# The norm's vector folded into the gate and value weights, and the factors of the tokens applied on ScalarE

## The chip, the core and the metric

The kernel runs on one core of one Trainium2 chip. The core has five engines with a queue of instructions each: TensorE (PE, matrix products, with its weight loads as PEld), VectorE (DVE), ScalarE (ACT), GpSimd (POOL), and SyncE (SP), which here only issues DMAs. An engine runs its queue in order and waits on semaphores for the others. The metric is the device time of one execution in microseconds (us). Before the change it is 991.82 us, the median of 3 runs (989.93 to 992.64).

## The reference

Three layers run one after the other over 2,304 tokens of width 512 (18 tiles of 128 tokens).

```python
x = attention(q, k, v)            # window of 128, 8 heads, a bias that falls with distance
# a layer of 8 experts, each token goes to its two best, with weights top2_w
for e in range(E):
    for k in range(2):
        h = np.maximum(x[mask] @ w1[e], 0.0)
        out[mask] += top2_w[mask, k, None] * (h @ w2[e])
# gated layer
rms = np.sqrt(np.mean(x * x, axis=-1, keepdims=True) + 1e-06)
xn = x / rms * rms_g
g = xn @ w_gate
silu = g * (1.0 / (1.0 + np.exp(-g)))
val = xn @ w_val
return (silu * val @ w_out).astype(np.float32)
```

The change concerns the step between the experts and the gated layer (the weighted sum of a token's two expert outputs, and the norm), and the preparation of `w_gate` and `w_val`.

## The kernel before

Products are made from two fp16 parts of each operand: a high part `hi` (ScalarE, a copy with a scale) and a rest `lo` (VectorE or GpSimd, a subtraction), three products of parts for one product.

**Stages.** Attention runs first, then the experts 0 to 7, with the experts' and the gated layer's weights split into parts beside the products. `m2_part` (L638 to L646) lists the 36 pieces of the gated layer's weights, `m2_steps` (L648) decodes and splits them: ScalarE writes `hi` at L658 with the scale `sc`, VectorE writes `lo` at L661. The gated layer then works on a first block of 2 token tiles (`FIRST`) and four blocks of 4 tiles (`QT`). The first block goes through `gated` (L853): 12 chunks f0 to f11 of 128 columns of the hidden width. The four later blocks go through `quads` (L965 to L1043), which needs fewer products but needs sums of weight blocks (`weight_sums`, L922: VectorE adds at L933, ScalarE copies at L936, GpSimd subtractions at L939). Most of these sums are made while the first block and the start of block 1 run.

**One chunk of `gated`.** TensorE makes the gate product and the value product (L875) into two PSUM rings, `mm0` with 3 buffers and `mm1` with 2. ScalarE writes silu of the gate product into a tile `gt` (even chunks) or `vt` (odd chunks), at L880. VectorE multiplies by the value product (L887), ScalarE copies that to `pgh` (L889), VectorE subtracts to `pgl` (L891). Each of `gt` and `vt` has one buffer, so silu of chunk f+2 waits for L891 of chunk f, and TensorE's value product of chunk f+2 waits for L887 of chunk f.

**Tokens for the next block.** `combine` (L792) runs for a block while the block before it is computed. In steps it gathers the two expert outputs of a token tile with two indirect DMAs of GpSimd (`ya`, `yb`, L758), then makes `ya*cw0` (L764) and `yb*cw1 + ya` (L765) on VectorE (`mixed`), the sum of squares on ScalarE (L719), the inverse root (L723 to L738), and for two pairs of tiles the norm (L741, VectorE: `ya*r*gb`, with `gb` the vector `rms_g` on all partitions, times 4), four additions (L818 to L821), fp16 parts (ScalarE L832, GpSimd L833) and transposing DMAs (L838). `combine_first` (L768) does this for the first block, one tile at a time, during the last expert, with a simpler end: norm, copy to fp16 (L746), a subtraction (L747), a transposing DMA (L748).

**What sets the order.** Everything is issued in the order in which the Python program writes it (`manual_schedule`). `drive` (L146) lets a main generator yield, and each yield tells how many columns TensorE was given. A side generator starts at a column count and then takes one step for each so many columns. `combine` of the first call starts `AHEAD[0]*PACE[0]` = 13*4,000 columns before the end of `gated`, later calls `AHEAD[1]*PACE[1]` = 9*8,000 columns before the end of a block's quads. `combine_first` has a pace of 3,100 columns, `weight_sums` one of 3,200.

Of the kernel before, what the change touches and what calls it, by code (L numbers as in the profile page):

```python
# [13 lines left out]
F32 = mybir.dt.float32  # L14
# [7 lines left out]
P = 128  # L22
# [5 lines left out]
MM = (3, 2)  # L28
VN = 96

AHEAD, PACE = (13, 9), (4000, 8000)

SOON, SUM0, SUMS = 3, 6000, 3200

# [7 lines left out]
def attention_moe_swiglu(  # L42
# [49 lines left out]
    over = consts.tile([P, 1], I32, name="over")  # L92
    tops = consts.tile([P, NT, 2], F32, name="tops")

    gb = consts.tile([P, DM], F32, name="gb")
    wts = {}

    def weight_steps(epools, stage, w1, w2, ws):
# [140 lines left out]
    with ExitStack() as actx:  # L239
# [169 lines left out]
        def constants():  # L409
            nc.vector.tensor_scalar(wgh, wg, SG, None, op0=OP.mult)  # L410
            nc.vector.scalar_tensor_tensor(wgl, wg, SG, wgh, op0=OP.mult, op1=OP.subtract)
            yield
            nc.vector.tensor_copy(bias[1], bias[0])
            nc.gpsimd.memset(bias[1][P // 2:, :, :P + P // 2], NEG * KS)
            yield
            nc.vector.tensor_copy(bias[2], bias[0])
            nc.gpsimd.memset(bias[2][:, :, :P // 2], NEG * KS)
            yield
            nc.gpsimd.memset(ones, 1.0)
            nc.gpsimd.memset(tri, 1.0)  # L420
            nc.gpsimd.affine_select(out=tri, in_=tri, compare_op=OP.is_gt, fill=0.0, base=0,
                                    pattern=[[1, P]], channel_multiplier=-1)
            nc.gpsimd.iota(iota8, pattern=[[1, E]], base=0, channel_multiplier=0,
                           allow_small_or_imprecise_dtypes=True)
            nc.vector.tensor_scalar(gb, gb, SN, None, op0=OP.mult)

            for e in range(E):
                yield
                nc.sync.dma_start(xrows[e * N + CAP - P:e * N + CAP, :], x16s[0].rearrange("p a d -> p (a d)"))
# [31 lines left out]
        def route(t0, nb):  # L461
# [49 lines left out]
            if t0 < 10:  # L511
# [6 lines left out]
            nc.vector.tensor_scalar(rank, rank, float(CAP - 1), None, op0=OP.min)  # L518
            nc.vector.scalar_tensor_tensor(ysl[:, ts, :], ixf, float(CAP), rank, op0=OP.mult, op1=OP.add)

        nc.sync.dma_start(gb, bass.AP(tensor=moe2_rms_g.tensor, offset=moe2_rms_g.offset,
                                      ap=[[0, P], [1, DM]]))
        few = work.tile([P, len(EARLY)], F32, name="few", bufs=1)

        def take(i, tiles, cs):
# [112 lines left out]
    def m2_part(i):  # L638

        if i < 6 * KC:  # L640
            m, j = divmod(i, 3 * KC)
            c, n0 = j // 3, j % 3 * DM
            src, sc = ((moe2_w_gate, SWG), (moe2_w_val, SWV))[m]
            return (src[c * P:(c + 1) * P, n0:n0 + DM], sc, *(x[:, c, n0:n0 + DM] for x in gw[2 * m:2 * m + 2]))
        c = i - 6 * KC
        return moe2_w_out[c * P:(c + 1) * P, :], SWO, ow[0][:, c, :], ow[1][:, c, :]  # L646

# [83 lines left out]
    def inverse(mp, vv, r):  # L731
        nc.vector.reciprocal(r, r)

        u = mp.tile([P, QT], F32, name="u")[:, :r.shape[1]]
        nc.vector.tensor_tensor(out=u, in0=vv, in1=r, op=OP.mult)
        nc.vector.tensor_tensor(out=u, in0=u, in1=r, op=OP.mult)
        nc.vector.tensor_scalar(u, u, -0.5, 1.5, op0=OP.mult, op1=OP.add)
        nc.vector.tensor_tensor(out=r, in0=r, in1=u, op=OP.mult)  # L738

    def normal(x3, r):  # L740
        nc.vector.scalar_tensor_tensor(x3, x3, r, gb, op0=OP.mult, op1=OP.mult)  # L741

    def turned(mp, x3, r, xnT, lo):
        normal(x3, r)
        xn = mp.tile([P, 2 * DM], F16, name="xg", bufs=3)
        nc.vector.tensor_copy(xn[:, :DM], x3)  # L746
        lo.tensor_tensor(out=xn[:, DM:], in0=x3, in1=xn[:, :DM], op=OP.subtract)  # L747
        nc.sync.dma_start_transpose(xnT, xn)  # L748

    def columns(xnT, i):  # L750
# [2 lines left out]
    def gather(mp, t, every=False):  # L753

        rows = yall if every else ybuf[:E * CAP if t >= G else (E - 1) * CAP + GW, :]
        ys = [mp.tile([P, DM], F32, name=name, bufs=bufs) for name, bufs in (("ya", QT), ("yb", 2))]
        for j, y in enumerate(ys):
            nc.gpsimd.indirect_dma_start(  # L758
                out=y, out_offset=None, in_=rows,
                in_offset=bass.IndirectOffsetOnAxis(ap=(slots if every else ysl)[:, t, j:j + 1], axis=0))  # L760
        return ys

    def mixed(t, ya, yb):
        nc.vector.tensor_scalar(ya, ya, cw[:, t, 0:1], None, op0=OP.mult)  # L764
        nc.vector.scalar_tensor_tensor(ya, yb, cw[:, t, 1:2], ya, op0=OP.mult, op1=OP.add)  # L765
        return ya

    def combine_first(mp, xnT):  # L768

        ys = [gather(mp, i) for i in range(FIRST)]  # L770
        for _ in range(WAIT):
            yield

        sqs = [mp.tile([P, 1], F32, name=f"sq{i}", bufs=1) for i in range(FIRST)]
        x3s, rs = {}, {}
        for n in range(2 * FIRST + 3):
            for i in range(FIRST):
                j = n - 2 * i
                if j == 0:
                    x3s[i] = mixed(i, *ys[i])  # L780
                elif j == 1:
                    square(mp, x3s[i], sqs[i])
                elif j == 2:
                    rs[i] = variance(mp, sqs[i])
                elif j == 3:
                    nc.scalar.activation(rs[i][1], rs[i][0], AF.Sqrt)
                elif j == 4:
                    inverse(mp, *rs[i])
                    turned(mp, x3s[i], rs[i][1], columns(xnT, i), nc.vector if i == FIRST - 1 else nc.gpsimd)
            yield  # L790

    def combine(mp, t0, xq):  # L792

        ys, x3s = {}, {}
        pairs = [(j, j + HQ) for j in range(HQ)]
        turn = list(itertools.chain(*pairs))
        sq = mp.tile([P, QT], F32, name="sq")
        for n in range(QT + 3):
            if n < QT:
                ys[n] = gather(mp, t0 + turn[n])  # L800
            if 0 <= n - 2 < QT:
                x3s[turn[n - 2]] = mixed(t0 + turn[n - 2], *ys[n - 2])
            if 0 <= n - 3:
                i = turn[n - 3]
                square(mp, x3s[i], sq[:, i:i + 1])
            yield
        vv, r = root(mp, sq)
        yield
        inverse(mp, vv, r)
        yield  # L810
        K2 = DM // 2
        for j, (a, b) in enumerate(pairs):
            xa, xb = x3s[a], x3s[b]
            tt = mp.tile([P, 3, K2], F32, name="tt", bufs=1)
            normal(xa, r[:, a:a + 1])
            normal(xb, r[:, b:b + 1])
            yield
            nc.vector.tensor_tensor(out=tt[:, 0], in0=xb[:, :K2], in1=xa[:, :K2], op=OP.subtract)  # L818
            nc.vector.tensor_tensor(out=xb[:, :K2], in0=xb[:, K2:], in1=xb[:, :K2], op=OP.subtract)
            nc.vector.tensor_tensor(out=tt[:, 1], in0=xb[:, K2:], in1=tt[:, 0], op=OP.subtract)  # L820
            nc.vector.tensor_tensor(out=tt[:, 2], in0=xa[:, K2:], in1=tt[:, 1], op=OP.subtract)  # L821
            yield
            parts = []
            for x in (xa, xb, tt[:, :2].rearrange("p k d -> p (k d)"), tt[:, 2]):
                n = x.shape[1] // K2
                if n == 2:
                    xn = mp.tile([P, 2 * DM], F16, name="xg", bufs=3)
                else:
                    xn = mp.tile([P, DM], F16, name="xh", bufs=1)
                y = xn.rearrange("p (k h d) -> p k h d", k=n, h=2)  # L830
                x = x.rearrange("p (k d) -> p k d", k=n)
                nc.scalar.activation(y[:, :, 0], x, AF.Copy)  # L832
                nc.gpsimd.tensor_tensor(out=y[:, :, 1], in0=x, in1=y[:, :, 0], op=OP.subtract)  # L833
                parts.append(xn)
            yield
            for k, xn in enumerate(parts):
                nb = xn.shape[1] // P
                nc.sync.dma_start_transpose(xq[:, 8 * k:8 * k + nb, j * P:(j + 1) * P], xn)  # L838
            yield

    def normalize(mp, x3s, xnT):
        sq = mp.tile([P, QT], F32, name="sq")[:, :G]
        for i, x3 in enumerate(x3s):
            square(mp, x3, sq[:, i:i + 1])
        vv, r = root(mp, sq)
        inverse(mp, vv, r)
        for i, x3 in enumerate(x3s):
            turned(mp, x3, r[:, i:i + 1], columns(xnT, i), nc.gpsimd)

    def products(ppool):  # L850
        return [ppool.tile([P, GC, QT * P], F16, name=name) for name in ("pgh", "pgl")]
# [243 lines left out]
    with tc.If(flag):  # L1095
        with ExitStack() as c:
# [18 lines left out]
            ph, pl = products(ppool)  # L1115
            for t in range(0, NT, G):
                xnT = xpool.tile([P, 2 * KC, GW], F16, name="xnT")
                normalize(mp, [mixed(t + i, *gather(mp, t + i, True)) for i in range(G)], xnT)
                for _ in itertools.chain(gated(mp, ph, pl, t, G, xnT), projected(ph, pl, t, G, range(GC))):
                    pass  # L1120

# [40 lines left out]
```

## Time and profile before

| | |
|---|---|
| median of 3 runs | 991.82 us |
| profiled execution, its own time | 997.68 us |
| its span, first to last instruction | 996.0 us |
| granted TensorE clock, mean | 0.986 |
| PE busy | 955.9 us (96%) |
| DVE busy | 656.4 us (66%) |
| ACT busy | 450.9 us (45%) |
| POOL busy | 212.0 us (21%) |

All rows come from one profiled execution; their times count from its first instruction. L and a number is a line of the kernel before. In a timeline or an issue order, `out<-in` names tiles. "Idle before, releaser" is the time in which an engine had nothing to run, and what ended it. The granted clock is a share of full speed: 1.00 is 2.4 GHz and 0.50 is 1.2 GHz. Attention takes about the first 165 us, the experts run up to 577.5 us, the first block of the gated layer runs to 634.6 us, and the four later blocks to the end.

### The profile page before, as it was taken

The numbers are of one execution on the slowest core, as the hardware profiler recorded it, in microseconds if no ns is written. First come the engines' busy times: TensorE is split into PE (matmuls) and PEld (weight loads), VectorE is DVE, ScalarE is ACT, GpSimd is POOL, SyncE is SP. The second block draws the span as 40 slices with busy tenths as digits, with TensorE's granted clock in tenths as the row PEclk, the third lists the DMA queues.
The fourth block names the chain that finished last, engine by engine and source line by source line (L and its number), as shares of the span: only waits on it lengthen the run. The fifth ranks groups of instructions, "written<-read, shape, count | busy, mean of one in ns | idle before, by whom it ended". The sixth has DMA issues, their size and how long they took to land.

```text
span 996.0 us, 18517 instructions
## 1 busy us (share of the span) xinstructions
PE 955.9 (96%) x7220; PEld 667.4 (67%) x7220; DVE 656.4 (66%) x1503; ACT 450.9 (45%) x920; POOL 212.0 (21%) x255
## 2 busy tenths in 40 slices
PE   7999987999999999999999998889999999999997
PEld 5998885655656565656565685578478658847864
DVE  6688864537666666667675479989548917954850
ACT  8999852434454545454543335335323413432320
POOL 5467643000000000000001355541401140130000
PEclk9999988999999999999999998999999999999999
DMA  7999664748484757575750232311341070122000
GB/s 217 307 239 287 145 186 138 198 131 229 153 227 164 217 170 215 160 206 167 218 149 22 75 105 51 69 53 33 73 98 33 9 161 1 33 60 59 1 13 34
DMA packets 145279, 127.12 MB, mean 128 GB/s; under 512 B 97696, under 2 KB 114848, under 8 KB 145184
## 3 DMA queue, kind: packets, MB, share of 16 engines
q1 hardware_dynamic: 139424, 106.99, 40.1%
q0 software_dynamic: 5760, 18.88, 5.8%
q8 instruction: 58, 0.95, 0.4%
q14 instruction: 37, 0.30, 0.1%
HBM read 76.81 MB, written 26.74 MB: 104 GB/s over the span
## 4 chain that ended last, share of the span: by engine, by line
PE 86%; DVE 7%; ACT 2%; DMA 2%; issue 1%; SPq 1%; another core or an unknown queue 0%; DVEq 0%; ACTq 0%
PE acc L210 21%; PE mm L189 21%; PE mm L982 21%; PE acc L909 11%; PE acc L361 6%; PE mm L347 3%; DVE sums L933 3%; PE mm L319 2%; DMA xq<-xg 1%; SPq L838 1%; PE mm L875 1%; DVE pgl L891 1%; DMA raw<-in_qkv 1%; PE rt L458 1%
## 5 line engine op out<-in xcount | busy, mean ns | idle before, releaser
L189 PE MATMUL mm<-xT,w1h 128*128 128x256 f16 (+2 forms) x1088 | 167.1, 294 | 1.1 <-issue 0.8
L195 DVE SCALAR_TENSOR_TENSOR hl<-mm,hh 128x256 f16<-128x256 f32 (+2 forms) x136 | 63.5, 469 | 118.8 <-ACT hh L194 117.6
L189 PEld LDWEIGHTS <-w1h 128*128 128x128 f16 x1088 | 104.8, 99 | 41.2 <-issue 2.6
L210 PE MATMUL acc<-w2h,hh 128*128 128x512 f16 x320 | 121.3, 379 | 0.0
L210 PE MATMUL acc<-w2l,hh 128*128 128x512 f16 x320 | 121.3, 379 | 0.0
L210 PE MATMUL acc<-w2h,hl 128*128 128x512 f16 x320 | 121.3, 379 | 0.0
L939 POOL TENSOR_TENSOR sw<-sums,sw 128x256 f16<-128x256 f32 x36 | 28.4, 809 | 391.8 <-ACT sw L936 391.8
L210 PEld LDWEIGHTS <-hh 128*128 128x128 f16 x640 | 62.6, 98 | 72.8
L982 PE MATMUL mm<-xq,sw 128*128 128x256 f16 x864 | 100.4, 273 | 2.4 <-DMA xq<-xg 2.3
L194 ACT ACTIVATE hh<-mm 128x256 f16<-128x256 f32 (+2 forms) x136 | 56.6, 419 | 92.2 <-PE mm L189 86.2
L982 PEld LDWEIGHTS <-sw 128*128 128x128 f16 x864 | 84.3, 98 | 13.0 <-issue 2.7
L189 PE MATMUL mm<-xT,w1l 128*128 128x256 f16 (+2 forms) x544 | 93.1, 293 | 0.0
L909 PE MATMUL acc<-oh__3183,pgl 128*128 128x512 f16 (+2 forms) x228 | 83.3, 368 | 1.6 <-DVE pgl L891 1.6
L909 PE MATMUL acc<-oh__3183,pgh 128*128 128x512 f16 (+2 forms) x228 | 83.3, 368 | 0.4 <-ACT pgh L889 0.4
L909 PE MATMUL acc<-ol__3184,pgh 128*128 128x512 f16 (+2 forms) x228 | 83.3, 368 | 0.0
L909 PEld LDWEIGHTS <-pgh 128*128 128x128 f16 x456 | 44.0, 98 | 49.1 <-ACT pgh L889 0.7
L361 PE MATMUL acc<-v,pf 128*128 128x96 f32 x544 | 73.8, 277 | 2.6 <-issue 2.4
L361 PEld LDWEIGHTS acc<-v,pf 128*128 128x128 f32 x544 | 69.3, 197 | 2.4 <-issue 2.4
L189 PEld LDWEIGHTS <-w1l 128*128 128x128 f16 x544 | 52.5, 99 | 18.1
L339 ACT ACTIVATE pr<-ss,nm 128x256 f32<-128x256 f32 (+1 forms) x144 | 63.1, 488 | 3.2 <-DVE nm L330 2.1
L330 DVE CUSTOM_DVE_ANT_0 ss<-mm,bias 128x256 f32<-128x256 f32 (+1 forms) x144 | 54.2, 397 | 15.2 <-PE mm L319 6.7
L232 ACT ACTIVATE ys<-acc 128x512 f32<-128x512 f32 x40 | 23.8, 594 | 82.7 <-PE acc L210 74.2
(190 smaller groups left out, 1729.0 us busy)
## 6 DMA issues: line engine op xcount, KB each, us to landing
st<-in_moe_w SPq DMA_DIRECT2D x64, 512.0 KB, 4.9
ybuf<-ys SPq DMA_DIRECT2D x40, 256.0 KB, 3.0
raw<-in_qkv SPq DMA_DIRECT2D x17, 512.0 KB, 5.5
st<-in_moe_w_gate SPq DMA_DIRECT2D x12, 512.0 KB, 4.7
st<-in_moe_w_val SPq DMA_DIRECT2D x12, 512.0 KB, 4.3
st<-in_moe_w_out SPq DMA_DIRECT2D x12, 512.0 KB, 4.4
v<-in_qkv SPq DMA_DIRECT2D x18, 279.0 KB, 5.6
out<-ys SPq DMA_DIRECT2D x17, 256.0 KB, 2.1
```

Source lines behind the costliest of these rows:

```text
L189: nc.tensor.matmul(hp[:, :w], w1[:, c, f * P:(f + 1) * P], xT[:, xo + c, cs], start=(n == 0), stop=(n == 3 * KC - 1))
L194: nc.scalar.activation(hh[:, f, hs], hp[:, :w], AF.Relu)
L195: nc.vector.scalar_tensor_tensor(hl[:, f, hs], hp[:, :w], 0.0, hh[:, f, hs], op0=OP.max, op1=OP.subtract)
L210: nc.tensor.matmul(yp, hx[:, f, i * P:(i + 1) * P], w2[:, f, :], start=(n == 0), stop=(n == 3 * FC - 1))
L330: nc.vector.tensor_tensor_reduce(out=d["ss"][:, j, c0:], in0=d["sp"][:, j, c0:], in1=bias[kind][:, heads(d["hp"])[j], c0:], scale=-1.0 / K ...
L339: nc.scalar.activation(d["pr"][:, j, c0:], d["ss"][:, j, c0:], AF.Exp, scale=-1.0, bias=d["nm"][:, j:j + 1])
L347: nc.tensor.transpose(pt[:, j, kk, :], d["pr"][:, j, kk * P:(kk + 1) * P], ident)
L361: nc.tensor.matmul(xps[t, hp // 2][:, h % 4, :VN], ph[:, j, kk, :], v32[t - 1 + kk][:, h * DV:h * DV + VN], start=(kk == k0), stop=(kk == 1))
L909: nc.tensor.matmul(op[:, ds], px[:, f, cs], w[:, f, ds], start=(k == 0), stop=(k == 3 * GC - 1))
L933: nc.vector.tensor_tensor(out=o, in0=x, in1=y, op=op)
L939: nc.gpsimd.tensor_tensor(out=here[k][1], in0=x, in1=here[k][0], op=OP.subtract)
L982: nc.tensor.matmul(pp, w(a, pa, c), xq[:, 4 * b + 2 * pb + c, :], start=(n == 0), stop=(n == 5))
```

## The change

The vector `rms_g` leaves the tokens. It is loaded as 128 x 4 (`gain[:, 0]`, one number for each row of a weight chunk), multiplied by the old constant scales `SWG` and `SWV`, and the 24 pieces of the gate and value weights take it as their scale, one number for each partition. The factor 4 (`SN`) of the tokens goes into the inverse root. The norm of a tile is then a factor for each token alone, and it moves from VectorE to ScalarE, as does the first factor of the weighted sum (`weighted`). In `combine_first` and in the spare path, ScalarE writes `hi` from `x3*r` directly, and VectorE writes `lo` as `x3*r - hi`; the separate norm, the copy and GpSimd's subtraction go. `combine` and `combine_first` have one step more, since `weighted` stands a step ahead of `mixed`; `AHEAD` grows by one each, so that `combine` starts a step earlier. `yb` has 3 buffers for 2.

```diff
-AHEAD, PACE = (13, 9), (4000, 8000)
+AHEAD, PACE = (14, 10), (4000, 8000)
...
-            nc.vector.tensor_scalar(gb, gb, SN, None, op0=OP.mult)
+            nc.vector.tensor_scalar(gain[:, 1], gain[:, 0], SWV, None, op0=OP.mult)
+            nc.vector.tensor_scalar(gain[:, 0], gain[:, 0], SWG, None, op0=OP.mult)
...
-        nc.sync.dma_start(gb, bass.AP(tensor=moe2_rms_g.tensor, offset=moe2_rms_g.offset,
-                                      ap=[[0, P], [1, DM]]))
+        nc.sync.dma_start(gain[:, 0], moe2_rms_g.rearrange("(c p) -> p c", p=P))
...
-            src, sc = ((moe2_w_gate, SWG), (moe2_w_val, SWV))[m]
-            return (src[c * P:(c + 1) * P, n0:n0 + DM], sc, *(x[:, c, n0:n0 + DM] for x in gw[2 * m:2 * m + 2]))
+            src = (moe2_w_gate, moe2_w_val)[m]
+            return (src[c * P:(c + 1) * P, n0:n0 + DM], gain[:, m, c:c + 1], *(x[:, c, n0:n0 + DM] for x in gw[2 * m:2 * m + 2]))
...
-        nc.vector.tensor_tensor(out=r, in0=r, in1=u, op=OP.mult)
-
-    def normal(x3, r):
-        nc.vector.scalar_tensor_tensor(x3, x3, r, gb, op0=OP.mult, op1=OP.mult)
-
-    def turned(mp, x3, r, xnT, lo):
-        normal(x3, r)
+        nc.vector.scalar_tensor_tensor(r, r, SN, u, op0=OP.mult, op1=OP.mult)
+
+    def turned(mp, x3, r, xnT):
         xn = mp.tile([P, 2 * DM], F16, name="xg", bufs=3)
-        nc.vector.tensor_copy(xn[:, :DM], x3)
-        lo.tensor_tensor(out=xn[:, DM:], in0=x3, in1=xn[:, :DM], op=OP.subtract)
+        nc.scalar.activation(xn[:, :DM], x3, AF.Copy, scale=r)
+        nc.vector.scalar_tensor_tensor(xn[:, DM:], x3, r, xn[:, :DM], op0=OP.mult, op1=OP.subtract)
         nc.sync.dma_start_transpose(xnT, xn)
...
-        ys = [mp.tile([P, DM], F32, name=name, bufs=bufs) for name, bufs in (("ya", QT), ("yb", 2))]
+        ys = [mp.tile([P, DM], F32, name=name, bufs=bufs) for name, bufs in (("ya", QT), ("yb", 3))]
...
+    def weighted(t, ya, yb):
+        nc.scalar.activation(ya, ya, AF.Copy, scale=cw[:, t, 0:1])
+
     def mixed(t, ya, yb):
-        nc.vector.tensor_scalar(ya, ya, cw[:, t, 0:1], None, op0=OP.mult)
         nc.vector.scalar_tensor_tensor(ya, yb, cw[:, t, 1:2], ya, op0=OP.mult, op1=OP.add)
         return ya
...
-        for n in range(QT + 3):
+        for n in range(QT + 4):
             if n < QT:
                 ys[n] = gather(mp, t0 + turn[n])
             if 0 <= n - 2 < QT:
-                x3s[turn[n - 2]] = mixed(t0 + turn[n - 2], *ys[n - 2])
-            if 0 <= n - 3:
-                i = turn[n - 3]
+                weighted(t0 + turn[n - 2], *ys[n - 2])
+            if 0 <= n - 3 < QT:
+                x3s[turn[n - 3]] = mixed(t0 + turn[n - 3], *ys[n - 3])
+            if 0 <= n - 4:
+                i = turn[n - 4]
                 square(mp, x3s[i], sq[:, i:i + 1])
...
-            normal(xa, r[:, a:a + 1])
-            normal(xb, r[:, b:b + 1])
+            for i in (a, b):
+                nc.scalar.activation(x3s[i], x3s[i], AF.Copy, scale=r[:, i:i + 1])
```

TensorE's order is the same before and after, and SP's differs in the one load of `rms_g`. Two places of the other engines follow. The first is VectorE's queue during the first block, from L891 of chunk f4 on; `ya` and `yb` are the gathered outputs, `sums` the sums of weight blocks. Before:

```order
L891 TENSOR_TENSOR pgl<-gt,pgh 128x256
L887 TENSOR_TENSOR vt<-vt,mm_7486 128x256
L933 TENSOR_TENSOR sums<-sums 128x256 x2
L764 TENSOR_SCALAR ya<-ya,cw 128x512
L765 SCALAR_TENSOR_TENSOR ya<-yb,cw,ya 128x512
L933 TENSOR_TENSOR sums<-vh__3181,sums 128x256
L933 TENSOR_TENSOR sums<-vl__3182,sums 128x256
L764 TENSOR_SCALAR ya<-ya,cw 128x512
L765 SCALAR_TENSOR_TENSOR ya<-yb,cw,ya 128x512
L891 TENSOR_TENSOR pgl<-vt,pgh 128x256
L887 TENSOR_TENSOR gt<-gt,mm_7532 128x256
```

After, from the pair of additions on:

```order
L936 TENSOR_TENSOR sums<-sums 128x256 x2
L764 SCALAR_TENSOR_TENSOR ya<-yb,cw,ya 128x512
L936 TENSOR_TENSOR sums<-vh__3182,sums 128x256
L936 TENSOR_TENSOR sums<-vl__3183,sums 128x256
L764 SCALAR_TENSOR_TENSOR ya<-yb,cw,ya 128x512
L894 TENSOR_TENSOR pgl<-vt,pgh 128x256
L890 TENSOR_TENSOR gt<-gt,mm_7532 128x256
```

The two products of `ya` with `cw` are gone, and nothing else has moved; the pairs of norms (`ya<-ya,r,gb`) further down are gone from this queue in the same way. The second place is ScalarE's queue a little later, around the table load between the root and the silu of chunk f9. Before:

```order
L728 ACT_TABLE_LOAD
L728 ACTIVATE r<-vv 128x4
L889 ACTIVATE pgh<-vt 128x256
L936 ACTIVATE sw_7249<-sums 128x256
L880 ACT_TABLE_LOAD
L880 ACTIVATE vt<-mm_7664 128x256
L936 ACTIVATE sw_7250<-sums 128x256
L889 ACTIVATE pgh<-gt 128x256
```

After:

```order
L729 ACT_TABLE_LOAD
L729 ACTIVATE r<-vv 128x4
L892 ACTIVATE pgh<-vt 128x256
L939 ACTIVATE sw_7248<-sums 128x256
L883 ACT_TABLE_LOAD
L883 ACTIVATE vt<-mm_7663 128x256
L939 ACTIVATE sw_7249<-sums 128x256
L819 ACTIVATE ya<-ya,r 128x512 x2
L892 ACTIVATE pgh<-gt 128x256
```

The pair of norms now stands on ScalarE between the silu of chunk f9 and the copy `pgh` of chunk f8.

## Rows read from the trace of the kernel before

**Rows 1.** Windows by stage: length, busy by engine, granted clock, DMA share, GB/s.

```profile
300.00:400.00 100.00, 100.00 (x594) 57.91 (x592) 67.17 (x119) 47.72 (x94) 0.00 (x0) 1.00 0.65 189
590.00:604.60 14.60, 10.21 (x93) 8.85 (x92) 13.40 (x24) 5.43 (x18) 10.02 (x11) 0.97 0.42 125
634.60:658.10 23.50, 17.90 (x158) 15.09 (x157) 22.78 (x39) 8.99 (x22) 12.25 (x16) 1.00 0.12 34
658.10:697.90 39.80, 39.80 (x349) 34.98 (x349) 35.39 (x57) 17.69 (x28) 8.56 (x9) 0.96 0.19 54
731.50:785.40 53.90, 53.90 (x493) 48.22 (x493) 44.39 (x69) 20.84 (x33) 2.84 (x3) 1.00 0.07 21
```

**Rows 2.** TensorE's longest waits from 576 to 664: total, times, longest.

```profile
PE mm L982 <- ACT p L1003: 4.1, 2, 2.1
PE mm L875 <- DVE gt L887: 3.1, 1, 3.1
PE acc L909 <- DVE pgl L891: 1.6, 1, 1.6
```

**Rows 3.** Chain that ended last, 590 to 698: start, length, what.

```profile
590.18 0.46 DVE ya L764
...
594.71 0.41 DVE ya L764
...
599.38 1.44 DVE ya L764
...
602.59 0.49 DVE ya L764
...
611.49 1.32 DVE ya L741 x2
...
623.62 1.33 DVE ya L741 x2
...
658.06 39.82 PE mm L982 x348
```

**Rows 4.** POOL's timeline: start, length, operation, idle before.

```profile
599.83 1.51 POOL L939 TENSOR_TENSOR hl<-sums,hl 128x256 f16<-128x256 f32 x2
```

**Rows 5.** VectorE's timeline: the first sum, and the product in a later block.

```profile
591.63 1.26 DVE L765 SCALAR_TENSOR_TENSOR ya<-yb,cw,ya 128x512 f32<-128x512 f32 x1 [0.99 <-DMA yb<-ybuf,ysl]
...
678.13 0.48 DVE L764 TENSOR_SCALAR ya<-ya,cw 128x512 f32<-128x512 f32 x1
```

**Rows 6.** ScalarE's timeline: the second table load, two copies to `pgh`.

```profile
610.44 1.28 ACT L880 ACT_TABLE_LOAD   x1 [1.18 <-DVE pgl L891]
...
612.32 0.41 ACT L889 ACTIVATE pgh<-gt 128x256 f16<-128x256 f32 x1
...
625.65 0.42 ACT L889 ACTIVATE pgh<-vt 128x256 f16<-128x256 f32 x1 [3.53 <-DVE vt L887]
```

**Rows 7.** VectorE's timeline, behind that copy.

```profile
612.76 0.87 DVE L891 TENSOR_TENSOR pgl<-gt,pgh 128x256 f16<-128x256 f32 x1
```

**Rows 8.** ScalarE's groups by shape: count, busy, mean ns, idle before.

```profile
L719 ACT ACTIVATE jk<-ya 128x512 f16<-128x512 f32 x18 | 11.2, 620 | 3.2 <-DVE ya L765 3.0
L339 ACT ACTIVATE pr<-ss,nm 128x256 f32<-128x256 f32 x128 | 57.7, 500 | 3.2 <-DVE nm L330 2.1 <-DVE rs L372 0.8
L1003 ACT ACTIVATE p<-mm 128x256 f32<-128x256 f32 x48 | 18.2, 380 | 81.4 <-PE mm L982 79.8 <-DVE vt L991 1.6
```

**Rows 9.** ScalarE's timeline in block 1: copies behind which the products wait.

```profile
675.64 0.38 ACT L1003 ACTIVATE p<-mm 128x256 f32<-128x256 f32 x1 [2.13 <-PE mm L982]
...
680.23 0.38 ACT L1003 ACTIVATE p<-mm 128x256 f32<-128x256 f32 x1 [0.91 <-PE mm L982]
...
684.81 0.38 ACT L1003 ACTIVATE p<-mm 128x256 f32<-128x256 f32 x1 [0.53 <-PE mm L982]
```

**Rows 10.** SP's timeline at the start: two loads and their issue times.

```profile
4.49 0.94 SPq L399 DMA_DIRECT2D wg<-in_moe_w_gate  x1
...
7.58 3.18 SPq L521 DMA_DIRECT2D gb<-in_moe_rms_g  x1
```

More of the change, by code (lines that the diff above doesn't have):

```diff
@@ L93, in attention_moe_swiglu @@
     tops = consts.tile([P, NT, 2], F32, name="tops")
-    gb = consts.tile([P, DM], F32, name="gb")
+    gain = consts.tile([P, 2, KC], F32, name="gain")
     wts = {}
@@ L775, in combine_first @@
         x3s, rs = {}, {}
-        for n in range(2 * FIRST + 3):
+        for n in range(2 * FIRST + 4):
             for i in range(FIRST):
-                j = n - 2 * i
-                if j == 0:
+                j = n - 2 * i - 1
+                if j == -1:
+                    weighted(i, *ys[i])
+                elif j == 0:
                     x3s[i] = mixed(i, *ys[i])
@@ L788, in combine_first @@
                     inverse(mp, *rs[i])
-                    turned(mp, x3s[i], rs[i][1], columns(xnT, i), nc.vector if i == FIRST - 1 else nc.gpsimd)
+                    turned(mp, x3s[i], rs[i][1], columns(xnT, i))
             yield
@@ L847, in normalize @@
         for i, x3 in enumerate(x3s):
-            turned(mp, x3, r[:, i:i + 1], columns(xnT, i), nc.gpsimd)
+            turned(mp, x3, r[:, i:i + 1], columns(xnT, i))
     def products(ppool):
@@ L1117, in attention_moe_swiglu @@
                 xnT = xpool.tile([P, 2 * KC, GW], F16, name="xnT")
-                normalize(mp, [mixed(t + i, *gather(mp, t + i, True)) for i in range(G)], xnT)
+                ys = [gather(mp, t + i, True) for i in range(G)]
+                for i in range(G):
+                    weighted(t + i, *ys[i])
+                normalize(mp, [mixed(t + i, *ys[i]) for i in range(G)], xnT)
                 for _ in itertools.chain(gated(mp, ph, pl, t, G, xnT), projected(ph, pl, t, G, range(GC))):
```

## The prediction

> **What bounds the kernel now.** I read the windows by stage first. From 300 to 400, with the experts at work, TensorE is busy all 100.00 us, and from 731.5 to 785.4 all 53.90 [rows 1]: there a us saved on VectorE or ScalarE returns nothing. From 634.6 to 658.1 it is otherwise: TensorE works 17.90 of 23.50 us and VectorE 22.78; from 590.0 to 604.6 TensorE has 10.21 of 14.60 and VectorE 13.40 [rows 1]. Next the waits of TensorE in that stretch: the three longest kinds, 4.1, 3.1 and 1.6 us, end with a copy `p` of ScalarE, the product L887 and the subtraction L891 of VectorE [rows 2]. So from about 590 to 658 VectorE's queue sets the pace. Last the chain of waits, which shows which of VectorE's instructions lie on the path: it holds the four products L764 and the four norms L741 of the first block's `combine`, until TensorE starts at 658.06 on 39.82 us of products without a stop [rows 3]. What VectorE loses before 658 moves the end; what it loses later doesn't.
>
> **The change, part by part.**
>
> First factors, 590 to 604. Four L764 leave VectorE: 0.46, 0.41, 1.44 and 0.49 us of the chain [rows 3]. The first returns nothing: the sum behind it then waited 0.99 us for the gather `yb` [rows 5], and that wait only becomes longer. The other three make 0.41 + 1.44 + 0.49 = 2.34. The 1.44 is a stretched one: a later one takes 0.48 [rows 5], and while this one ran GpSimd was at two subtractions, 599.83 to 601.34 [rows 4]. If the stretch of 0.96 passes to the neighbour, 2.34 - 0.96 = 1.38 are left; if the gather comes earlier too, 2.34 + 0.46 = 2.80. I take 2.34, the rows as they stand.
>
> The Trainium skill speaks against that value (GPSIMD Engine Reference, Key points): GpSimd and VectorE share their way into SBUF, and contend where a VectorE instruction has two SBUF inputs or uses two ports. The trace agrees that the product is three times as long beside GpSimd [rows 4, 5]. By that rule the neighbour, a sum with two inputs, inherits the stretch, and the total below would be 1.9 in place of 2.9, so 989.9 us.
>
> On ScalarE each factor now stands in front of a copy `pgh` or a silu, waits there until `ya` has landed, and holds what is queued behind it, for which L891 waits. `ya` is the gather before `yb` and lands earlier; its wait is bounded by none and by the 0.99 seen for `yb` [rows 5]. VectorE has sums of its own to do meanwhile, and I count nothing; without that cover it is up to 0.99.
>
> What such an operation costs on ScalarE isn't shown, since it reads its scale for each partition. A 128x512 one with a constant takes 620 ns; on 128x256, one with a bias for each partition takes 500 and one without 380 [rows 8]. So between 0.62 and 0.62 + 0.12 = 0.74 us; I take 0.74, as the row with a pointer is nearest in kind.
>
> Norms of the first pair of tiles, near 612. 1.32 us leave the chain [rows 3], but this is the place where little comes back. ScalarE loads a table at 610.44, then does a silu and a copy, and `pgh` of chunk f8 runs from 612.32 to 612.73; L891, which needs it, starts at 612.76 [rows 6, 7]. VectorE's two norms fitted under that table load. Without them VectorE arrives 1.32 us earlier and waits. And the two norms on ScalarE are issued between that silu and that `pgh`, which puts `pgh` 2 x 0.74 = 1.48 later. So this pair is worth between -1.48 (all of it a wait) and +1.32 (ScalarE has run ahead far enough). The rows put it near the lower end, because `pgh` and L891 lie 0.03 apart; L891 took a stretched 0.87 there [rows 7] and may run freely when it comes later, so I take -0.8.
>
> Norms of the second pair, near 623.6. 1.33 us leave [rows 3]. ScalarE's two stand before `pgh` of f11, in front of which ScalarE was idle 3.53 us for VectorE [rows 6]; 1.48 fit in. The full 1.33 counts; bounds 0 and 1.33.
>
> Edits at nothing. (a) `combine_first` comes one step of 3,100 columns later. With 348 x 256 columns in 39.82 us [rows 3] that is 1.4 us, and its tail loses a norm and a copy on VectorE. If it comes late, TensorE starts the first block up to 1.4 later, and its waits of 4.1 + 3.1 + 1.6 [rows 2] take that in. (b) The 24 weight pieces with a scale for each partition: 24 x 0.12 = 2.9 us more on ScalarE, in a stage where it is busy 47.72 of 100 and TensorE all 100.00 [rows 1]; uncovered, 2.9. (c) The load of `rms_g` becomes 512 runs of four bytes: its issue lies between 0.94 (the load of `wg`, 512 runs) and the 3.18 of the old one [rows 10]. No step of the chain waits on it; SP reaches the next loads up to 2.2 earlier, which nobody is late for. (d) In the three later runs of `combine`, 4 products at 0.48 and 4 norms of about 0.67 each leave VectorE beside a TensorE without a gap [rows 1, 3, 5]: 3 x 4.6 = 13.8 us less work and no time. (e) Gathers are issued a step earlier and `yb` has a third buffer; GpSimd's queue keeps the same gathers and weight subtractions, two of them in turned order, and loses one subtraction of `combine_first`. SP's queue passes nothing.
>
> The sum: 2.34 - 0.8 + 1.33 = 2.9 us. The profiled execution took 997.68 us for a span of 996.0; it would take 994.8. It lies 5.9 us above the median of the runs, 991.82, from which the same 2.9 leave **988.9 us**.
>
> **The rivals.**
>
> R1, VectorE's saving comes back whole. For it: VectorE is 97% busy from 634.6 to 658.1 (22.78 of 23.50), ScalarE 38% (8.99) [rows 1], so ScalarE may run ahead in the chunks before. Against it: the 0.03 us between `pgh` and L891 [rows 6, 7]. It gives 2.34 + 1.32 + 1.33 = 5.0, so 986.8. If TensorE's clock also stays up behind 658, where 39.8 us were granted 0.96, 39.8 x 0.04 = 1.6 more: 985.2.
>
> R2, ScalarE and GpSimd hand most of it back: the stretch passes on and the first pair is all wait, 1.38 - 1.48 + 1.33 = 1.2, so 990.6; with the waits of the factors for `ya`, nothing. For it: rows 4 and 6. Against it: ScalarE idles long in most chunks (the 3.53 of rows 6).
>
> R3, slower: ScalarE falls behind in the blocks where TensorE has no gap. There two factors come in front of one copy `p`, and one each in front of the next two; the copy waits for TensorE's product with 2.13, 0.91 and 0.53 us of idle time before it [rows 9]. At 0.74 each nearly all fits (1.48, 0.74 and 0.74 against these: 0.21 late). If the moved operations were stretched as L764 was, to 1.44, it would be 0.75 + 0.53 + 0.91 = 2.2 us late a block. Should TensorE feel all of it in three blocks, 6.6 - 2.9 = 3.7 slower: 995.5. It turns slower from about 1.1 us an operation, at which (0.07 + 0.19 + 0.57) x 3 = 2.5 are lost, and all has to reach TensorE. Against it: 18 ScalarE operations of this size take 620 ns in the mean [rows 8], none like 1.44. The Trainium skill has a rule of this kind (ScalarE: Activation LUTs, Rules for kernel authors): multiplications belong on VectorE, not on ScalarE. The trace agrees on the price, 0.48 against 0.62 to 0.74 [rows 5, 8]; by the rule the change loses, by the rows only where ScalarE is the later engine.
>
> **How the numbers follow.** I give the forecast 0.48 (987.4 to 990.4), R1 0.22, R2 0.19 and R3 0.11. What a measurement of this kernel can tell from no change is about 0.3%, here 3.0 us, and the forecast sits on that edge: half of its chance counts as faster. Faster is 0.24 + 0.22 = 0.46, the same 0.24 + 0.19 = 0.43, slower 0.11. The range takes in R1 with the better clock and R2 down to no gain, 985.2 to 991.8, and leaves out R3 and a little at the lower end.
>
> **What would show it.** In the changed kernel's profile, the start on the long run of block 1's products (658.06 before) should lie about 3 us earlier. L891 of chunk f8 should wait 1 to 2.5 us for `pgh` on VectorE, with the two norms just before that `pgh` on ScalarE; without that wait R1 holds. From 590 to 604 TensorE should wait about 2 us less for L887. The last four blocks should keep their lengths (53.9 us of quads each); if one grows by over a us, with TensorE waiting for `p`, R3 holds. A stage before 577 us that changes by over a us would make the whole account wrong, as would a stretch up to 658 that stays as long while VectorE idles less than 3 us more.

## The result, and the profile after

The changed kernel is slower: 1000.22 us, the median of 20 runs (992.78 to 1011.4), against 992.97 us for 20 runs of the kernel before; the ratio is 1.0066, 95% interval 1.0049 to 1.0082. One of the 20, that of 1011.4, was in a slow state of the chip and is left out of the ratio. The forecast was 988.9 us, with a range of 985.2 to 991.8.

The profiled execution took 1003.16 us for a span of 1001.1. To compare it with that of before, the part ahead of the gated layer has to be set aside. First the first gated product of each, before and then after:

```profile
577.54 0.39 PE L875 MATMUL mm<-xq,gh 128*128 128x128 f16 x4
```

```profile
573.51 0.39 PE L878 MATMUL mm<-xq,gh 128*128 128x128 f16 x4
```

The 4.03 us between them arise ahead of the experts' second layers: the first product of an expert's second layer comes at 177.30 and 173.27, and from there to the first gated product both take 400.24. In the other profiled executions below the first gated product lies between 569.73 and 576.11, so this part scatters and is no gain. Everything below is counted from the first gated product: 418.46 us to the end before (996.0 - 577.54), 427.59 after. That is 9.1 us more.

The chain of waits of the changed kernel (start, length, what) shows where they are; `xq` are the transposed tokens of the next block. It answers to [rows 3]:

```profile
588.75 4.42 DMA ya<-ybuf,ysl
...
593.20 0.72 ACT ya L761
...
608.68 1.22 ACT ya L819 x2
609.90 0.32 ACT pgh L892
610.24 0.43 DVE pgl L894
...
653.84 38.15 PE mm L985 x348
691.99 23.32 PE acc L912 x108
...
720.15 9.48 DMA xq<-xg
...
729.68 56.04 PE mm L985 x492
785.72 23.32 PE acc L912 x108
...
814.01 8.38 DMA xq<-xg
...
822.44 55.54 PE mm L985 x492
877.98 31.08 PE acc L912 x144
```

and the same part of the chain before, behind the last of [rows 3]:

```profile
697.87 23.32 PE acc L909 x108
...
726.22 5.22 DMA xq<-xg
...
731.49 53.87 PE mm L982 x492
785.36 23.32 PE acc L909 x108
...
813.62 5.17 DMA xq<-xg
...
818.83 53.87 PE mm L982 x492
```

From the first gated product to the long run of 348 products it took 80.52 us before (658.06 - 577.54) and 80.33 after (653.84 - 573.51): of the 2.9 us forecast, 0.2 came. The 348 products took 38.15 instead of 39.82, 1.7 less, because the clock stayed up (granted 1.00 there, against the 0.96 of [rows 1]). The loss lies behind: from the end of a block's quads to the next block's it took 33.62 us before (731.49 - 697.87) and 37.69 after, then 33.47 and 36.72. That is 4.07 + 3.25 us, and the products behind the two waits took 2.17 and 1.67 longer. The sum is -0.19 - 1.67 + 4.07 + 2.17 + 3.25 + 1.67 = 9.3, against the 9.1 counted. TensorE's longest waits from 560 to the end (total, times, longest), which answer to [rows 2]:

```profile
PE mm L985 <- DMA xq<-xg: 9.6, 2, 5.3
PE mm L985 <- ACT p L1006: 4.3, 2, 2.3
PE mm L878 <- DVE vt L890: 3.9, 2, 2.6
```

The first kind was 2.3 us in two waits before. The wait of 5.3 us ended at 729.68, and the first 4.5 us of products behind it ran at 1.2 GHz (windows; columns as in [rows 1]):

```profile
728.00:730.00 2.00, 0.32 (x2) 0.25 (x2) 0.00 (x0) 0.00 (x0) 0.00 (x0) 0.50 1.06 199
730.00:732.00 2.00, 2.00 (x12) 1.34 (x10) 0.69 (x1) 0.00 (x0) 0.00 (x0) 0.50 0.00 0
732.00:734.00 2.00, 2.00 (x11) 1.40 (x10) 0.28 (x1) 0.00 (x0) 0.00 (x0) 0.50 0.00 0
734.00:736.00 2.00, 2.00 (x20) 1.74 (x19) 1.51 (x3) 0.03 (x1) 0.00 (x0) 0.96 0.03 8
```

Why does a transpose (L841) for the next block take 9.48 us to land, and 5.22 before? GpSimd's timeline at that place, first and last gather of the run, before:

```profile
718.80 0.97 POOL L758 DMA_INDIRECT ya<-ybuf,ysl  x1
...
723.82 0.95 POOL L758 DMA_INDIRECT ya<-ybuf,ysl  x1 [0.30 <-issue]
```

and after:

```profile
712.92 0.96 POOL L755 DMA_INDIRECT ya<-ybuf,ysl  x1 [0.15 <-issue]
...
720.47 0.95 POOL L755 DMA_INDIRECT ya<-ybuf,ysl  x1 [0.30 <-issue]
```

Before, five gathers go out in a row, one each 1.25 us, until the third `yb` finds no buffer. After, with three buffers, seven do. SP issues the transposes meanwhile, behind the store of the third output tile, from 722.27 before and from 716.39 after: in both kernels 3.5 us behind the first gather. So the transposes share the DMA engines with two gathers more. That is theory T1. The trace shows the two queues side by side: from 724 to 726 in the changed kernel the gathers' packets took 39.5% of the DMA engines' time and those of SP's queue 91.1%. The transposes for the last block, beside which no gathers run, land some 3.3 us after their issue. The Trainium skill has a rule that fits (DMA: Bandwidth & Descriptors, Queues, rings and completion order): each DMA engine serves the queues that have work for it in turn, a packet at a time. By it a gather in flight takes turns from a transpose, and the trace agrees: 3.3 us without gathers, 5.2 behind five, 8.4 and 9.5 behind seven.

In the first block, ScalarE's timeline (line, operation, and in brackets the idle time before and its releaser):

```profile
593.20 0.72 ACT L761 ACTIVATE ya<-ya,cw 128x512 f32<-128x512 f32 x1 [2.95 <-DMA ya<-ybuf,ysl]
...
608.58 1.32 ACT L819 ACTIVATE ya<-ya,r 128x512 f32<-128x512 f32 x2
609.81 0.40 ACT L892 ACTIVATE pgh<-gt 128x256 f16<-128x256 f32 x1
```

and VectorE's, for the two `pgh` behind them:

```profile
594.87 0.95 DVE L894 TENSOR_TENSOR pgl<-gt,pgh 128x256 f16<-128x256 f32 x1 [1.67 <-ACT pgh L892]
...
610.24 0.43 DVE L894 TENSOR_TENSOR pgl<-gt,pgh 128x256 f16<-128x256 f32 x1 [2.49 <-ACT pgh L892]
```

A factor waits 2.95 us for its gather and holds `pgh`, so VectorE waits 1.67; later the two norms hold `pgh`, and VectorE waits 2.49.

### The profile page after: what moved, and what is told of

It is laid out like the page before. It is cut to its first block, busy times and chain, and to the rows that moved or that the text cites. A ratio compares the mean times of both kernels' runs of the same rounds, so it can differ in the third digit from the quotient of the medians.

```text
span 1001.1 us, 18512 instructions
## 1 busy us (share of the span) xinstructions
PE 955.1 (95%) x7220; PEld 666.6 (67%) x7220; DVE 634.0 (63%) x1467; ACT 475.1 (47%) x956; POOL 208.1 (21%) x254
## 4 chain that ended last, share of the span: by engine, by line
PE 82%; DVE 7%; DMA 4%; issue 2%; ACT 2%; POOL 1%; SPq 1%; DVEq 0%; ACTq 0%; POOLq 0%
PE mm L985 21%; PE mm L190 19%; PE acc L211 19%; PE acc L912 11%; PE acc L362 5%; PE mm L348 3%; PE mm L320 3%; DVE sums L936 2%; DMA xq<-xg 2%; DMA ya<-ybuf,ysl 1%; SPq L841 1%; DMA raw<-in_qkv 1%; PE mm L878 1%; DVE pgl L894 1%; DVE ss L331 1%
## 5 line engine op out<-in xcount | busy, mean ns | idle before, releaser
L985 PE MATMUL mm<-xq,sw 128*128 128x256 f16 x864 | 105.6, 281 | 9.6 <-DMA xq<-xg 9.6
L985 PEld LDWEIGHTS <-sw 128*128 128x128 f16 x864 | 87.1, 101 | 22.6 <-issue 10.0
L994 DVE TENSOR_TENSOR gt<-mm,p 128x512 f32<-128x512 f32 x24 | 16.6, 690 | 77.5 <-PE mm L985 75.3
```

What stands on the lines that cost most here:

```text
L985: nc.tensor.matmul(pp, w(a, pa, c), xq[:, 4 * b + 2 * pb + c, :], start=(n == 0), stop=(n == 5))
```

## The experiments

The table has the lengths from the first gated product to the long run of 348 products and to the end, TensorE's waits for `xq` (of these in brackets the ones at block 1's start), the median and the ratio to the kernel before on the same chip (its medians lie between 992.11 and 993.47 there) with its 95% interval. Lengths are of one profiled execution each.

| run | to the long run | to the end | waits for xq | median us | ratio |
|---|---|---|---|---|---|
| before | 80.52 | 418.46 | 2.3 | 992.97 | |
| changed | 80.33 | 427.59 | 9.6 | 1000.22 | 1.0066 (1.0049 to 1.0082) |
| after_yb2 | 79.89 | 415.68 | 2.1 | 992.12 | 0.9996 (0.9984 to 1.0008) |
| norms_yb3 | 80.02 | 426.96 | 8.6 | 998.71 | 1.0062 (1.0042 to 1.0082) |
| norms_only | 80.13 | 417.87 | 2.3 | 991.81 | 0.9985 (0.9968 to 1.0002) |
| after_step | 77.11 | 415.17 | 4.3 (1.8) | 988.70 | 0.9964 (0.9948 to 0.9981) |
| after_early | 80.07 | 415.36 | 0 | 989.83 | 0.9971 (0.9955 to 0.9986) |
| before_early | 80.53 | 414.33 | 0 | 989.20 | 0.9970 (0.9959 to 0.9980) |
| before_later | 80.54 | 416.44 | 5.2 (3.5) | 992.48 | 1.0006 (0.9993 to 1.0020) |
| before_later_early | 80.79 | 416.23 | 3.4 (3.4) | 991.56 | 0.9979 (0.9965 to 0.9992) |
| first_step_early | 76.37 | 409.98 | 1.6 (1.6) | 987.23 | 0.9950 (0.9935 to 0.9965) |
| factor_late | 79.63 | 420.84 | 0 | 996.17 | 1.0021 (1.0005 to 1.0038) |
| hybrid_early | 79.21 | 414.29 | 0 | 988.92 | 0.9952 (0.9936 to 0.9967) |
| first_step_early_hyb | 77.72 | 412.82 | 1.6 (1.6) | 987.89 | 0.9931 (0.9907 to 0.9956) |

### The third buffer: after_yb2, norms_yb3, norms_only

```diff
-        ys = [... (("ya", QT), ("yb", 3))]      # after_yb2: the changed kernel with
+        ys = [... (("ya", QT), ("yb", 2))]
```

> The changed kernel with two yb buffers in place of three; all else stays. Theory T1 (the third yb buffer lets GpSimd issue 7 gathers in a row at a block's end, in place of 5, and they slow the transposes of xq for which TensorE waits): 5 gathers in a row again; the last transpose lands 5 to 6 us after its issue, not 8 to 9.5; TensorE waits 1 to 1.5 us for xq at each of two boundaries, not 4 to 5.3; no half clock behind them; 990 to 994 us, 6 to 10 below the changed kernel's 1000.2. Rival T2 (the cost comes with the earlier step or with ScalarE's added work in the blocks): the waits for xq stay at 4 to 5 us and the time at 997 to 1003.

TensorE's waits and, from the chain, the transpose at the first of the two boundaries:

```profile
PE mm L985 <- DMA xq<-xg: 2.1, 2, 1.3
```

```profile
721.29 5.04 DMA xq<-xg
```

As T1 said: five gathers, 5.04 us, and 11.9 us less to the end (427.59 to 415.68); the medians lie 8.1 us apart (1000.22 and 992.12), since the profiled execution was 2.9 us over its median in the changed kernel and 0.8 here. The reverse is a pair that differs in this buffer alone; both have the factors on VectorE:

```diff
-        nc.scalar.activation(ya, ya, AF.Copy, scale=cw[:, t, 0:1])
+        nc.vector.tensor_scalar(ya, ya, cw[:, t, 0:1], None, op0=OP.mult)
...                         # in the step of the sum; AHEAD (13, 9); yb 3 (norms_yb3) or 2 (norms_only)
```

> The fold and the norms on ScalarE, the factors of the tokens back on VectorE in the step of the sum as before, AHEAD as before, but three yb buffers. T1 (third buffer): 7 gathers in a row, waits for xq of 4 to 5 us at two boundaries, 997 to 1003 us. T2 (the earlier step, or the factors on ScalarE): waits of 1 to 1.5 us, 990 to 994. In the first block both theories expect the two L741 of the first pair to return nothing (VectorE waits for pgh) and those of the second pair 1.3 us.

> The fold and the norms on ScalarE, the factors of the tokens on VectorE in the step of the sum, AHEAD (13, 9), two yb buffers: the change without its first factors and without the third buffer. Lengths are counted from the first gated product, since the part ahead of it differs from execution to execution by some us. T1: five gathers, waits for xq of 1 to 1.4 us at two boundaries; from the first gated product to the long run of block 1's products 80.0 us (80.5 before): -0.8 for the first pair of norms, +1.3 for the second; to the end 415.5 to 417 (418.5 before); 990.5 to 992.5 us. Rival: the norms hold more on ScalarE than one pgh; then the stretch is over 80.5 and the time over 993.

The waits of norms_yb3:

```profile
PE mm L984 <- DMA xq<-xg: 8.6, 2, 5.5
```

The two waits were 3.1 and 5.5 us, where T1 had said 4 to 5. 998.71 us with three buffers and 991.81 with two. No factor runs on ScalarE in either, and AHEAD is that of before: T1 holds, and neither the factors on ScalarE nor the earlier step is needed for the loss. norms_only's 80.13 is near the 80.0 expected for the norms alone. Its 417.87 lies above the range; at the start of the long run the granted clock fell to 0.71 (649.8 to 653.0), as it did in the kernel before.

### The step and the order at a block's end: after_step, after_early, before_early

```diff
-AHEAD, PACE = (14, 10), (4000, 8000)      # after_step
+AHEAD, PACE = (13, 9), (4000, 8000)
```

> The changed kernel with AHEAD back at (13, 9): the same work, each step of combine is written one step later; three yb buffers. T1 (third buffer): GpSimd issues its gathers as soon as buffers are free, whatever step they are written in, so 7 in a row stay, waits for xq of 4 to 5 us stay, 997 to 1003 us. T2 in its form with the earlier step: waits back at 1 to 1.5 us, 990 to 994.

A miss of T1 as it was written: 988.70 us, with three buffers and seven gathers. The waits at the two boundaries were 1.1 and 1.4 us, as the rival T2 had them, and the time lay below both ranges. GpSimd's and SP's timelines at the block's end say why:

```profile
715.75 0.97 POOL L755 DMA_INDIRECT ya<-ybuf,ysl  x1
```

```profile
712.78 3.97 SPq L841 DMA_TRANSPOSE xq<-xg  x3
```

The gathers follow GpSimd's last subtraction of `combine`, and a later step delays that subtraction (L836), here until the store ahead of the transposes was out. So the transposes were issued 3 us ahead of the first gather instead of 3.5 us behind it. T1 has to be put more exactly: what counts is how many gathers are issued ahead of the last of the transposes (L841), not how many there are. In norms_yb3, with the same AHEAD but no step of its own for the factors, the first gather again stands 3.5 us ahead of them (713.87 and 717.35), and the waits are there. The second kernel tests that from the other side:

```diff
                 parts.append(xn)
-            yield
             for k, xn in enumerate(parts):
...
                 nc.sync.dma_start_transpose(xq[...], xn)
             yield
+            yield
```

> The changed kernel with the transposes of a pair written one step earlier, so that in SP's queue the second pair's stand ahead of the store of a block's third output tile instead of behind it; three yb buffers. T1: seven gathers still run beside the transposes, which still take 8 to 10 us, but these are issued about 4 us earlier, so the wait for xq of 4 to 5.3 us falls to 0 to 1.5 a boundary: 988 to 993 us. T2 with ScalarE's added work as the cause: TensorE is as late by another wait, 997 to 1003.

SP's timeline:

```profile
713.68 3.99 SPq L840 DMA_TRANSPOSE xq<-xg  x3
```

Its first gather came at 716.65. Seven gathers, three buffers, AHEAD (14, 10), and no wait for `xq`: 989.83 us. The last of these transposes landed 4.8 us after its issue, not 8 to 10 as T1 had said: all three were issued ahead of the gathers, and some 5 us earlier than in the changed kernel. This run alone can't tell which of the two removes the wait; after_yb2, where the order and the time of issue stay, can. The same edit in the kernel before:

> The kernel before with the transposes of a pair written one step earlier, ahead of the store of the third output tile in SP's queue. If the boundary is set by what stands ahead of the transposes: no wait for xq at both boundaries (1.2 us each before), 2.3 to 2.5 us less after the first block, 989 to 990.5 us. If the transposes are bound by their data instead, the waits stay and the time stays at 992.

989.20 us: the two waits of 1.2 and 1.1 us that the kernel before had there go too.

### The first block: before_later, before_later_early, first_step_early, factor_late

after_step also took 3.4 us off the way to the long run, against the kernel before. Was it the moved work, or only the later step?

```diff
-AHEAD, PACE = (13, 9), (4000, 8000)      # before_later: the kernel before with
+AHEAD, PACE = (12, 9), (4000, 8000)
```

> The kernel before, with combine for block 1 written one step of 4,000 columns later (AHEAD 12 for 13); nothing is moved to ScalarE. Theory A (the changed kernel with AHEAD back gained 3.4 us in the first block because ScalarE's factors then found ya landed and held no pgh): the kernel before has no such factors, its first sum still waits about 1 us less for yb, so 79.5 to 80.5 us to the long run of block 1's products (77.1 in that run, 80.5 before), 991 to 993 us. Rival B (the step itself brings it, because sums, norms and GpSimd's subtractions meet otherwise): 77 to 78.5 us, 988 to 990 us.

80.54 us, at the edge of A's range and far from B's, but not cleanly. In its first block the last `pgl` came 46.01 us after the first gated product (48.56 before), and that gain then went into a wait at block 1's start:

```profile
635.00 2.79 PE L982 MATMUL mm<-xq,sw 128*128 128x256 f16 x24 [3.06 <-DMA xq<-xg]
```

So two kernels were run whose sums stand in the same step, with early transposes: AHEAD (12, 9) without the change, and (13, 10) with it.

> The kernel before with combine for block 1 one step later (AHEAD 12, 9) and the transposes one step earlier: the same schedule as the changed kernel with AHEAD (13, 10) and early transposes, which took 76.4 us to the long run of block 1's products, 410.0 to the end and 987.2 us, but without the change. Theory A (the moved factors and norms bring most of the first block's gain once ya has landed): 79 to 80.5 us, 413 to 414.5 to the end, 989 to 990.5. Rival B (the step brings it; the kernel before with the step alone lost its 2.5 us again at waits for xq): 76.5 to 78 us, 410 to 412 to the end, 987 to 988.5.

> The changed kernel with AHEAD (13, 10), that is the old step for block 1 and the new one for the later blocks, and with the transposes one step earlier; three yb buffers. Theory A and T1 together: 77.1 us to the long run of block 1's products, no waits for xq, 412 to 413 us from the first gated product to the end (427.6 in the changed kernel), 985.5 to 988 us. If one of the two gains is not what it seemed, 988 to 991.

80.79 without the change, 76.37 with it; 991.56 and 987.23 us. B is ruled out: the step alone brings nothing to the long run. But before_later_early also lies above all of A's ranges, by 0.3, 1.7 and 1.1 us. And the two schedules are not quite one: the change gives the factor a step of its own, so its gathers stand a step further ahead of the sums. The first gather comes 9.25 us after the first gated product with the change and 11.31 without, and two of VectorE's sums then wait for `yb` without the change, against one of 0.55 with it:

```profile
591.62 1.29 DVE L765 SCALAR_TENSOR_TENSOR ya<-yb,cw,ya 128x512 f32<-128x512 f32 x1 [0.70 <-DMA yb<-ybuf,ysl]
...
599.43 1.13 DVE L765 SCALAR_TENSOR_TENSOR ya<-yb,cw,ya 128x512 f32<-128x512 f32 x1 [1.01 <-DMA yb<-ybuf,ysl]
```

So the 4.4 us belong to the change together with its step; how much the moved work alone brings is not shown, since the kernel before with such a step was not run. The two were timed on different chips, and by their ratios (0.9979 and 0.9950) they lie 0.3% apart, some 2.9 us. first_step_early's chain from there on is TensorE without a gap:

```profile
650.29 38.15 PE mm L985 x348
688.44 31.08 PE acc L912 x144
719.52 55.02 PE mm L985 x504
774.54 31.08 PE acc L912 x144
```

The last one writes only the factor later, in the step of the sum (with early transposes):

```diff
-            if 0 <= n - 2 < QT:
-                weighted(t0 + turn[n - 2], *ys[n - 2])
             if 0 <= n - 3 < QT:
+                weighted(t0 + turn[n - 3], *ys[n - 3])
                 x3s[turn[n - 3]] = mixed(t0 + turn[n - 3], *ys[n - 3])
```

> The changed kernel with early transposes, and the first factor written in the step of the sum, one step later than in the change; AHEAD (14, 10). Theory A: ScalarE no longer waits for ya in front of pgh, so the fifth subtraction pgl of the first block comes 20.4 us or earlier after the first gated product (20.8 with early transposes, 21.4 in the changed kernel), and the long run of block 1's products starts 77.5 to 79.5 us after it (80.1); 987 to 989 us. Rival: VectorE's sum now waits for the factor instead, and VectorE's queue behind it: 80 to 81.5 us, 989.5 to 991.5.

The fifth `pgl` came at 19.40 us, as A had it (21.36 in the changed kernel), and the long run at 79.63, just past A's range. The whole was slower, 996.17 us, which neither theory had said; the place is the later blocks. VectorE's timeline there, and TensorE's waits from 660 to 1000:

```profile
679.27 0.75 DVE L764 SCALAR_TENSOR_TENSOR ya<-yb,cw,ya 128x512 f32<-128x512 f32 x1 [1.74 <-ACT ya L761]
```

```profile
PE mm L984 <- DVE gt L993: 3.9, 6, 0.7
PE mm L984 <- DVE vt L993: 2.1, 3, 1.2
```

VectorE's sum waits for the factor on ScalarE, the additions L993 stand behind the sum, and TensorE waits for them. In the changed kernel its longest waits in that stretch are for `xq` alone.

### The norms: hybrid_early, first_step_early_hyb

```diff
             for i in (a, b):
-                nc.scalar.activation(x3s[i], x3s[i], AF.Copy, scale=r[:, i:i + 1])
+                if j == 0:
+                    nc.vector.tensor_scalar(x3s[i], x3s[i], r[:, i:i + 1], None, op0=OP.mult)
+                else:
+                    nc.scalar.activation(x3s[i], x3s[i], AF.Copy, scale=r[:, i:i + 1])
```

> The fold with the factors of the tokens on VectorE, of the norms only the second pair on ScalarE and the first pair on VectorE (a product with one number for each token), AHEAD (13, 9), two yb buffers, early transposes. If the first pair's loss is the pgh behind it (norms on ScalarE put pgh 1.3 us later, and VectorE waited 2.5 us for it): the ninth pgl comes 35.0 to 35.3 us after the first gated product (35.2 before, 36.5 with both pairs on ScalarE), the long run of block 1's products after 79.0 to 79.5 (80.1 with both pairs moved), the end after 412.8 to 413.5; 988 to 989.5 us. If it is not: 36.5 and 80.1, and 989.5.

The ninth `pgl` of VectorE, with both pairs on ScalarE (norms_only) and with the second alone (hybrid_early):

```profile
606.26 0.43 DVE L893 TENSOR_TENSOR pgl<-gt,pgh 128x256 f16<-128x256 f32 x1 [2.49 <-ACT pgh L891]
```

```profile
611.35 0.70 DVE L896 TENSOR_TENSOR pgl<-gt,pgh 128x256 f16<-128x256 f32 x1 [0.48 <-ACT pgh L894]
```

From the first gated products (569.73 and 576.11) that is 36.53 and 35.24 us, and the long run begins at 79.21: both as expected, so the first pair's loss is the `pgh` behind it. The length to the end, 414.29, missed its range by 0.8: TensorE's clock fell at the start of the long run here (0.66 granted from 655.3 to 659.0), and not in before_early.

> The changed kernel with AHEAD (13, 10) and early transposes, and the first pair of norms on VectorE. In that schedule the first pair's norms stand on ScalarE behind the pgh that VectorE waits for, not ahead of it, so both theories of the first pair expect little: 76.0 to 77.0 us to the long run of block 1's products (76.4 with both pairs on ScalarE), 409.5 to 411 to the end, 986.5 to 988 us.

77.72 and 412.82, 1.4 and 2.8 more than with both pairs on ScalarE, over both ranges. Of the 1.4, half lies ahead of the moved norms (the eighth `pgl` came at 29.98 and at 30.67), and of the 2.8, 1.7 is the clock at the start of the long run (39.82 us for the 348 products, 38.15 with both pairs). Its median, 987.89, was as expected. It and first_step_early (987.23) were timed beside different runs of the kernel before, and their ratios overlap; which is better stays open. Both beat the kernel before and the changed one.

## Why the prediction was wrong

**The third buffer (edit e): wrong, and the cause of the miss.** I counted the same gathers in the same queue and put it at nothing. The buffer doesn't add a gather, it lets two more go out ahead of the last transposes, for which TensorE already waited 1.2 and 1.1 us at the two boundaries. The waits were in the trace, and I took the blocks from 658 on as bound by TensorE alone. With the clock that went with it, this is 11.9 us in the profiled executions (after_yb2), 0.4 of it ahead of the long run, and 8.1 us between the medians. No rival named it. R3 had the right sign with another place: its sign came, a block's quads longer by over a us (56.04 and 55.54 against 53.87), but TensorE never waited for ScalarE in the later blocks. Without the third buffer the change is still not worth its 2.9 us: after_yb2 takes as long as the kernel before (ratio 0.9996). That part of the miss is the next term.

**First factors: wrong.** 2.34 us forecast. The seventh `pgl` of the first block came at 28.69 us before and at 28.98 after: -0.3. In after_yb2 and after_early, with the same factors, it came at 28.56 and 28.71, so the term is about nothing. The step that failed is "its wait is bounded by none and by the 0.99 seen for `yb`": the factor waited up to 2.95 us for `ya` and held `pgh`. It is written a step ahead of the sum, but the gathers hardly came earlier: GpSimd issues the first one behind the same subtractions of `weight_sums`, 9.25 us after the first gated product before and 9.46 after, and the later ones at most 0.8 us earlier.

```profile
586.79 0.97 POOL L758 DMA_INDIRECT ya<-ybuf,ysl  x1 [0.15 <-issue]
```

```profile
582.97 0.97 POOL L755 DMA_INDIRECT ya<-ybuf,ysl  x1
```

So VectorE's four sums, freed of their products, still started between 0.5 us later and 0.4 us earlier than before. TensorE's waits for VectorE's products up to 604 didn't fall by the 2 us named either: 2.61 + 1.85 in the changed kernel, 1.31 + 3.08 before. R2 had this outcome in its last words ("with the waits of the factors for `ya`, nothing"), and I gave it too little. A step later part of it comes: the seventh `pgl` at 27.17 with the change and at 28.96 without (first_step_early, before_later_early).

**First pair of norms: right.** -0.8 forecast. From the seventh to the ninth `pgl` it took 6.53 us before and 7.75 after, 1.22 more; the `pgl` itself ran in 0.43 instead of the 0.87 of [rows 7], so 0.44 came back: -0.8. VectorE waited 2.49 us for `pgh`, inside the 1 to 2.5 given. hybrid_early shows the cause.

**Second pair: right.** 1.33 forecast. From the ninth `pgl` to the twelfth it took 13.34 us before (35.22 to 48.56) and 11.63 after: 1.71, of which 0.44 is the `pgl` counted above: 1.3.

**The price on ScalarE: right.** 0.74 taken, between 0.62 and 0.74. Its groups by shape (count, busy, mean ns, idle before), which answer to [rows 8]:

```profile
L761 ACT ACTIVATE ya<-ya,cw 128x512 f32<-128x512 f32 x18 | 12.5, 711 | 5.0 <-DMA ya<-ybuf,ysl 5.0
L819 ACT ACTIVATE ya<-ya,r 128x512 f32<-128x512 f32 x16 | 10.6, 708 | 0.0
```

**Edits a to c: right.** 400.24 us from the experts' second layers to the first gated product, before and after.

**The stretch beside GpSimd.** I kept the rows as they stood. The sums took 816 ns in the mean before and 822 after, over 18 each. The four of the first block, which are the ones that count, took 3.8 us together before and 4.2 after: some 0.4 more, of the 0.96 that could have passed to them. The page named in the prediction (the Trainium skill, GPSIMD Engine Reference, Key points) has sums with two SBUF inputs contend with GpSimd, and the trace agrees: after the change the three that took 1.07, 1.19 and 1.17 us each overlapped a subtraction of GpSimd, and the fourth, of 0.74, did not.

## What to carry to other kernels

A buffer more is an order of transfers: look at what the queue behind it can now issue, and whether something that the bottleneck waits for is issued after it on the same DMA engines. A wait of 1 us for a transfer at a boundary is a warning to price every change there, even if the engines are idle. Work moved to an idle engine that works in order brings its own wait with it and puts it ahead of what already stood there; let its input land first, as first_step_early does. Moving it later without more room in front of its reader only hands the wait on: factor_late lost it to VectorE's sum.

## What the runs showed of the hardware

- The wait of 5.3 us at the boundary cost TensorE 2.2 us more behind it: 492 products in 56.04 us, against 53.87 behind a wait of 1.2 us, after which the granted clock stayed at 1.00.
- The same wait of 2.00 us ahead of the 348 products was followed by 1.2 GHz in some profiled executions (39.82 us) and by 2.4 GHz in others (38.15). Which of them it is was not settled.
- The last transpose of `xq` (L838 before) landed 3.3 us after its issue with no gathers beside it, 4.9 to 5.3 us behind five, and 7.0 to 9.7 us behind seven (before, after_yb2, norms_only and before_later against the changed kernel and norms_yb3).
- VectorE's sum of 128x512 took 0.74 to 0.75 us wherever no subtraction of GpSimd overlapped it (202 of 252 sums in the profiled executions); every longer one had such an overlap.
- The part ahead of the gated layer differs by up to 7.8 us between profiled executions (569.73 to 577.54). Between these two all of it lies ahead of the experts' second layers; in hybrid_early the part behind took 401.60 us, not 400.24. Only lengths counted from behind it could tell steps of 1 us apart.
